# Packed attention and a low-rank MoE mixer on one core: GpSimd scales w1's high words, p is turned by plain products, and w2's first low part goes to VectorE

## The chip, the cores and the metric

The kernel runs on one core of a Trainium2 chip. The metric is the device time of one execution in microseconds (us); lower is better. A core has TensorE (matrix products, called PE in the profile, its weight loads PEld), VectorE (DVE), ScalarE (ACT), GpSimd (POOL) and SyncE (SP), which here issues nearly all transfers. Each engine works through its own queue in order; engines wait for each other and for transfers by semaphores.

## The reference, cut to what matters

```python
# q, k, v: (8, 8, 576, 64) float32   p: (8, 8, 32, 64) float32
p_packed = softmax(scale * p @ k^T) @ v            # 32 packed tokens per head
out      = softmax(scale * q @ p_packed^T) @ p_packed
x  = out as (8, 576, 512)
u  = x + (x^T @ U @ V)^T                           # U (576, 32), V (32, 576), float64 in memory
ch = max(u @ w_ch1, 0) @ w_ch2                     # w_ch1 (512, 2048), w_ch2 (2048, 512), float64 in memory
result = u + ch                                    # float32
```

The four weight arrays are float64 in memory. [...]

## The kernel before, in words

**Two parts.** The first part (lines 509 to 576, about the first 100 us) computes the packed attention of all 8 batches, converts w1 and does batch 0's second attention; a unit there is half a batch, four heads, and there are 16 units. Its instructions are put in order by the framework: with `schedule_with_timeline_sim=True` it simulates the program and gives each engine and each queue one fixed order. The second part (from line 579, `manual_schedule`) is the main loop. Its order is that in which the code is written. For each batch it goes over 16 tiles kt of the hidden width: `gemm1` (h_ps, with the folded first weight wth/wtl), the eviction with ReLU into a high and a low part (hh by ScalarE, hl by VectorE), and `gemm2` of the tile before (o, with w2h/w2l). Each product of these is three passes over high and low parts (`mm3`, L87 to L89). The bank of `h_ps` is single per half, so a tile's first product waits until the hl of the tile before has read it.

**w1.** 16 pieces of 128x512 are loaded by SP as pairs of words (`load_w1`, 512 KB each, four buffers, two named bits and two bits2), scaled (`test_w1`, L150, ScalarE: the high word read as a float32 and multiplied by 2 to the power of -112), and then shifted and joined by VectorE (`float32_of`, L80 to L82). `some_w1(n)` converts piece n, scales piece n+1 and loads piece n+4 into the buffer that n held. `fold` (L384) multiplies batch 0's packed tokens with w1; its results are evicted by ScalarE (wth, L390) and VectorE (wtl, L391).

**w2.** 16 tiles kt of 128x512, loaded into the two buffers `bits`, scaled by ScalarE (L79), joined by VectorE, and split into a high part (w2h, L165, ScalarE) and the rest (w2l, L166). Tiles 0, 1 and 2 are loaded late in the first part, tile 0 is converted and split there; its w2l is made by GpSimd, those of all other tiles by VectorE. The other tiles are converted between the steps of the main loop.

**p.** For each batch `a_load` brings p (pn, one buffer), and `a_p` turns it: GpSimd writes it twice side by side (pd, L433), TensorE transposes the two groups (L435), and ScalarE evicts them with the scale into pT: one copy for group 0 (L436), two for group 1, whose two halves change places within each pair of heads (L439). Then, for each unit: `a_turn` turns k (k_ps, kT), `a_scores` multiplies (L249, s_ps), `a_softmax` takes the maxima (L460, VectorE) and the exponentials (L462, ScalarE), `a_turn_back` turns them back (m_ps, eT, L471), `a_pack` multiplies with v (L490) and `a_heads` turns the result (L500). GpSimd also copies each result into ppall (L493) and does parts of the second attention (L290, L301, L347).

The order in which one unit is handled:

```python
a_turn_back(i - 1, ...); a_scores(i); a_load_v(i + 1); a_turn(i + 1); a_load(i + 2); a_softmax(i)
... some_w1(n_w1) ...
a_pack(i - 2, ...); a_heads(i - 3)
```

Of the kernel before, what the change touches and what calls it, by code (L numbers as in the profile page):

```python
# [9 lines left out]
F32 = mybir.dt.float32  # L10
F32R = mybir.dt.float32r
I32 = mybir.dt.int32
AF = mybir.ActivationFunctionType
ALU = mybir.AluOpType
# [6 lines left out]
def packed_attention_mixer_kernel(  # L21
# [27 lines left out]
    nc = tc.nc  # L49
    B, H, S, D = q.shape  # L50
# [4 lines left out]
    P = 128  # L55
# [7 lines left out]
    scale = 1.0 / float(D) ** 0.5  # L63
# [4 lines left out]
    REBIAS = 2.0 ** -112  # L68
    SIGN = -0x80000000

    U, V, w1, w2 = (a.bitcast(I32) for a in (U, V, w1, w2))
# [26 lines left out]

    ident = const.tile([P, P], F32, name="ident")
    make_identity(nc, ident)  # L100
    eps = const.tile([P, 1], F32, name="eps")
    nc.gpsimd.memset(eps, 1e-9)
    ppall = const.tile([P, B, 2, D], F32, name="ppall")
# [35 lines left out]
    bits = {}  # L139
# [6 lines left out]
    tests = {}  # L146

    def test_w1(n):
        tests[n] = conv_tile(F32)
        nc.scalar.activation(tests[n], bits["w1", n][:, :, 1].bitcast(F32), AF.Abs, scale=REBIAS)  # L150

    def convert_w1(n):
        x, c = chunks[n]
# [9 lines left out]
    def split_w2(kt, x):  # L163
        hi, lo = w2_parts(kt)
        nc.scalar.copy(hi, x)  # L165
        (nc.gpsimd if kt == 0 else nc.vector).tensor_tensor(lo, x, hi.bitcast(F32), op=ALU.subtract)  # L166

# [240 lines left out]
    def a_load(u):  # L410
        b, g = UN[u]
        ua[u] = {}
        if g == 0:
            pn[b] = sA.tile([P, 2, D], F32, name="pn", bufs=1)
            nc.sync.dma_start(out=pn[b], in_=p[b].rearrange("(g h) n d -> (h n) g d", g=2))
        ua[u]["x"] = sA.tile([P, 2 * S], F32, name="kx", bufs=3)
        load_nat(ua[u]["x"], k, b, g)
# [11 lines left out]
    def a_p(b):  # L429
        t_ps = bank()  # L430
        pT[b] = sA.tile([P, 2, P], F32, name="pT")
        pd = sA.tile([P, 2, 2, D], F32, name="pd", bufs=1)
        nc.gpsimd.tensor_copy(pd, pn[b].unsqueeze(2).to_broadcast([P, 2, 2, D]))  # L433
        for i in range(2):
            nc.tensor.transpose(t_ps[:, P * i:P * i + P], pd[:, i].rearrange("p z d -> p (z d)"), ident)  # L435
        nc.scalar.activation(pT[b][:, 0], t_ps[:, :P], AF.Copy, scale=scale)  # L436
        dst, src = (a.rearrange("p (y z n) -> p z y n", y=2, z=2) for a in (pT[b][:, 1], t_ps[:, P:2 * P]))
        for z in range(2):
            nc.scalar.activation(dst[:, z], src[:, 1 - z], AF.Copy, scale=scale)  # L439

    def a_turn(u):
        b, g = UN[u]
# [350 lines left out]
```

## Time and profile before

| | us |
|---|---|
| median of 3 runs | 831.68 (831.53 to 833.7) |
| the profiled execution | 831.53 |
| its span in the trace | 829.7 |
| TensorE busy | 798.7 |
| VectorE busy | 351.2 |
| ScalarE busy | 318.7 |
| GpSimd busy | 80.1 |
| first product of the main loop | 103.53 after the span's start |

The profile's page gives the busy time of each engine, a chain of waits followed back from the last instruction, and groups of equal instructions with their mean duration; `L87` is line 87 of the kernel before. Lines 101 to 432 of the kernel before have numbers higher by four in the kernel after (its L253 is L249 here), and from line 440 on they are the same. "x16" counts instructions; a plain float32 product leaves two of them in the trace. A view by stretches gives, for each stretch of time, the busy time of every engine, the clock that TensorE was granted (1.00 is full speed) and the share of time in which the 16 DMA engines worked.

### The profile page before, as it was taken

The page shows a single profiled execution, that of the slowest core. Times are in us where ns is not written, and L with a number is a line of the kernel's source. Part 1 is how long each engine was busy: PE and PEld are TensorE (multiplying, and loading weights), DVE is VectorE, ACT ScalarE, POOL GpSimd, SP SyncE. Part 2 cuts the span into 40 slices and gives each one's busy share as a digit, 9 for nine tenths or more (in the row PEclk, how much of TensorE's full clock was granted, in tenths as well). Part 3 has the DMA queues.
Part 4 walks back from the last instruction along what each step waited for, and adds up shares of the span by engine and source line. Part 5 has one row for each costly group of instructions (what it writes and reads, how often), then busy time and mean ns, then how long its engine had stood idle before and what let it go on. Part 6 is the DMA issues. An engine that isn't in the chain of part 4 may idle for free.

```text
span 829.7 us, 15436 instructions
## 1 busy us (share of the span) xinstructions
PE 798.7 (96%) x6224; PEld 643.7 (78%) x6224; DVE 351.2 (42%) x781; ACT 318.7 (38%) x974; POOL 80.1 (10%) x115
## 2 busy tenths in 40 slices
PE   7879698999999999999999999999999999999997
PEld 5556377888788888888888888888888888887886
DVE  3777467773343323433433234333434234332232
ACT  5788664354333332333333232343234232332231
POOL 0222201100111001010011001010101011100000
PEclk8999899999999999999999999999999999999999
DMA  9999764216001220023002120122002200030001
GB/s 299 347 360 358 252 139 127 78 51 188 1 1 47 100 55 2 1 96 92 1 1 89 58 55 2 46 87 57 2 18 90 73 22 1 14 111 1 2 0 64
DMA packets 60310, 70.23 MB, mean 85 GB/s; under 512 B 22864, under 2 KB 41296, under 8 KB 60240
## 3 DMA queue, kind: packets, MB, share of 16 engines
q1 hardware_dynamic: 59920, 68.73, 26.5%
q8 instruction: 49, 0.80, 0.4%
q10 hardware_dynamic: 320, 0.52, 0.2%
q14 instruction: 21, 0.17, 0.1%
HBM read 53.64 MB, written 15.60 MB: 83 GB/s over the span
## 4 chain that ended last, share of the span: by engine, by line
PE 89%; DVE 4%; DMA 3%; ACT 2%; issue 1%; POOL 0%; SPq 0%; ACTq 0%; POOLq 0%
PE o L87 16%; PE o L89 16%; PE o L88 16%; PE h_ps L87 9%; PE h_ps L89 8%; PE h_ps L88 8%; PE t_ps L384 4%; DMA bits<-in_moe_w_ch_dram 2%; PE o L654 2%; PE t_ps L229 2%; DMA vt<-in_v_dram 1%; PE t_ps L327 1%; PE t_ps L249 1%; PE t_ps L255 1%; DVE os L81 1%
## 5 line engine op out<-in xcount | busy, mean ns | idle before, releaser
L87 PE MATMUL o<-w2h,hh 128*128 128x512 f32 x512 | 206.6, 404 | 0.0
L89 PE MATMUL o<-w2h,hl 128*128 128x512 f32 x512 | 202.4, 395 | 0.0
L88 PE MATMUL o<-w2l,hh 128*128 128x512 f32 x512 | 201.9, 394 | 0.0
L637 DVE SCALAR_TENSOR_TENSOR hl<-h_ps,hh 128x256 fp32r<-128x256 f32 x256 | 105.4, 423 | 204.0 <-ACT hj L636 189.9
L634 ACT ACTIVATE hh<-h_ps 128x256 fp32r<-128x256 f32 x256 | 98.6, 386 | 182.9 <-PE h_ps L89 182.5
L87 PE MATMUL h_ps<-ah,wth 128*128 128x320 f32 (+1 forms) x512 | 157.7, 308 | 0.4 <-DVE hl L637 0.3
L88 PE MATMUL h_ps<-al,wth 128*128 128x320 f32 (+1 forms) x512 | 151.6, 296 | 0.0
L89 PE MATMUL h_ps<-ah,wtl 128*128 128x320 f32 (+1 forms) x512 | 151.5, 296 | 0.0
L87 PEld LDWEIGHTS h_ps<-ah,wth 128*128 128x128 f32 x512 | 96.7, 189 | 25.6 <-issue 21.0
L89 PEld LDWEIGHTS o<-w2h,hl 128*128 128x128 f32 x512 | 96.4, 188 | 22.5
L87 PEld LDWEIGHTS o<-w2h,hh 128*128 128x128 f32 x512 | 97.0, 189 | 21.0 <-issue 4.6
L88 PEld LDWEIGHTS o<-w2l,hh 128*128 128x128 f32 x512 | 97.0, 189 | 16.6
L88 PEld LDWEIGHTS h_ps<-al,wth 128*128 128x128 f32 x512 | 96.9, 189 | 1.9
L89 PEld LDWEIGHTS h_ps<-ah,wtl 128*128 128x128 f32 x512 | 97.0, 189 | 0.0
L391 DVE TENSOR_TENSOR wtl<-t_ps,wth 128x256 fp32r<-128x256 f32 x128 | 48.5, 420 | 102.4 <-ACT wth L390 99.0
L390 ACT CAST wth<-t_ps 128x256 fp32r<-128x256 f32 x128 | 43.3, 374 | 110.0 <-PE t_ps L384 102.3
L347 POOL TENSOR_TENSOR al<-aT,ah 128x320 fp32r<-128x320 f32 (+1 forms) x32 | 25.7, 806 | 211.5 <-ACT ah L346 211.5
L290 POOL TENSOR_TENSOR e<-e,m 128x576 f32<-128x576 f32 x16 | 18.6, 1160 | 261.8 <-DVE m L289 261.8
L236 ACT COPY xT<-t_ps 128x256 f32<-128x256 f32 x64 | 21.5, 395 | 38.9 <-PE t_ps L229 38.2
L384 PE MATMUL t_ps<-w1t,ppT 64*32 64x512 f32 x512 | 35.9, 615 | 0.0
L346 ACT CAST ah<-aT 128x320 fp32r<-128x320 f32 (+1 forms) x32 | 13.8, 435 | 43.8 <-DVE aT L345 43.8
L636 ACT ACTIVATE hj<-h_ps 128x64 f32<-128x64 f32 x128 | 28.3, 221 | 0.0
(121 smaller groups left out, 822.3 us busy)
## 6 DMA issues: line engine op xcount, KB each, us to landing
bits<-in_moe_w_ch_dram SPq DMA_DIRECT2D x32, 512.0 KB, 6.4
kx<-in_k_dram SPq DMA_DIRECT2D x16, 576.0 KB, 7.0
x<-in_q_dram SPq DMA_DIRECT2D x16, 576.0 KB, 5.0
vt<-in_v_dram SPq DMA_DIRECT2D x32, 256.0 KB, 6.9
out_dram<-bits SPq DMA_DIRECT2D x32, 256.0 KB, 2.4
aD<-aT SPq DMA_DIRECT2D x16, 288.0 KB, 2.1
aP<-aD SPq DMA_DIRECT2D x32, 128.0 KB, 3.4
ppP<-ppD SPq DMA_DIRECT2D x32, 64.0 KB, 3.1
```

Source lines behind the costliest of these rows:

```text
L87: nc.tensor.matmul(ps, lhsT=lh, rhs=rh, start=start, stop=False)
L88: nc.tensor.matmul(ps, lhsT=lh, rhs=rl, start=False, stop=False)
L89: nc.tensor.matmul(ps, lhsT=ll, rhs=rh, start=False, stop=stop)
L236: nc.scalar.copy(dst, src[:, a])
L290: nc.gpsimd.tensor_tensor(e, e, m.unsqueeze(2).to_broadcast([P, S // 32, 32]), op=ALU.subtract)
L347: nc.gpsimd.tensor_tensor(al[:, g, ns], aT[:, ns], ah[:, g, ns].bitcast(F32), op=ALU.subtract)
L384: nc.tensor.matmul(f_ps[g][xs], lhsT=ppT[b][zs, g, xs], rhs=w1t[h // 2][zs, QW * c:QW * c + QW], start=True, stop=True)
L390: nc.scalar.copy(hi[:, g], f_ps[g][:, cs])
L391: nc.vector.tensor_tensor(lo[:, g], f_ps[g][:, cs], hi[:, g].bitcast(F32), op=ALU.subtract)
L634: nc.scalar.activation(hh[:, ms], src, AF.Relu)
L636: nc.scalar.activation(hj[:, jslot(self.b, kt), self.js], h_ps[:, LAST], AF.Relu)
L637: nc.vector.scalar_tensor_tensor(hl[:, ms], src, 0.0, hh[:, ms].bitcast(F32), op0=ALU.max, op1=ALU.subtract)
```

## The change

Three edits, in the first part only. First, `test_w1` runs on GpSimd as a multiplication in place of ScalarE's absolute value with scale. The sign that this keeps is shifted out by the next step. Second, `a_p` no longer doubles and transposes p: it multiplies pn (as the stationary operand) with the identity for group 0 and with a new constant `swapped`, an identity with exchanged halves, for group 1, each once into the upper and once into the lower 64 rows of the bank; so the result stands in its final order and one ScalarE instruction evicts it. pd is gone and pn has two buffers. Third, w2's first low part is made by VectorE like the others.

```diff
+    swapped = const.tile([P, P], F32, name="swapped")
+    for z in range(2):
+        a, b = (x.rearrange("p (y z n) -> p z y n", y=2, z=2) for x in (swapped, ident))
+        nc.gpsimd.tensor_copy(a[:, z], b[:, 1 - z])
...
     def test_w1(n):
         tests[n] = conv_tile(F32)
-        nc.scalar.activation(tests[n], bits["w1", n][:, :, 1].bitcast(F32), AF.Abs, scale=REBIAS)
+        nc.gpsimd.tensor_single_scalar(tests[n], bits["w1", n][:, :, 1].bitcast(F32), REBIAS, op=ALU.mult)
...
     def split_w2(kt, x):
         hi, lo = w2_parts(kt)
         nc.scalar.copy(hi, x)
-        (nc.gpsimd if kt == 0 else nc.vector).tensor_tensor(lo, x, hi.bitcast(F32), op=ALU.subtract)
+        nc.vector.tensor_tensor(lo, x, hi.bitcast(F32), op=ALU.subtract)
...
-            pn[b] = sA.tile([P, 2, D], F32, name="pn", bufs=1)
+            pn[b] = sA.tile([P, 2, D], F32, name="pn", bufs=2)
...
     def a_p(b):
         t_ps = bank()
         pT[b] = sA.tile([P, 2, P], F32, name="pT")
-        pd = sA.tile([P, 2, 2, D], F32, name="pd", bufs=1)
-        nc.gpsimd.tensor_copy(pd, pn[b].unsqueeze(2).to_broadcast([P, 2, 2, D]))
-        for i in range(2):
-            nc.tensor.transpose(t_ps[:, P * i:P * i + P], pd[:, i].rearrange("p z d -> p (z d)"), ident)
-        nc.scalar.activation(pT[b][:, 0], t_ps[:, :P], AF.Copy, scale=scale)
-        dst, src = (a.rearrange("p (y z n) -> p z y n", y=2, z=2) for a in (pT[b][:, 1], t_ps[:, P:2 * P]))
-        for z in range(2):
-            nc.scalar.activation(dst[:, z], src[:, 1 - z], AF.Copy, scale=scale)
+        for i, z in product(range(2), range(2)):
+            nc.tensor.matmul(t_ps[D * z:D * z + D, P * i:P * i + P], lhsT=pn[b][:, i], rhs=(ident, swapped)[i],
+                             start=True, stop=True)
+        nc.scalar.activation(pT[b].rearrange("p g n -> p (g n)"), t_ps[:, :2 * P], AF.Copy, scale=scale)
```

Since the framework orders the first part anew, the edits move instructions on every engine. Three places follow. From the first product of the main loop on, the order of every engine is the same as before.

GpSimd's queue at the end of the first part, before (al is the low part of batch 0's second attention):

```order
L347 TENSOR_TENSOR al<-aT_918,ah 128x256
L347 TENSOR_TENSOR al<-aT_1122,ah 128x256
L493 COPY ppall<-two 128x64
L166 TENSOR_TENSOR w2l_103<-os,w2h_102 128x512
L433 COPY pd<-pn 128x256
```

and now:

```order
L154 TENSOR_SCALAR os<-bits_1410 128x512
L351 TENSOR_TENSOR al<-aT_911,ah 128x320
L493 COPY ppall<-two 128x64
L351 TENSOR_TENSOR al<-aT_1113,ah 128x320
L154 TENSOR_SCALAR os<-bits 128x512
L351 TENSOR_TENSOR al<-aT_911,ah 128x256
```

w2l and the copy of the last p, which stood behind it, are gone; the scaling of the last two pieces of w1 stands between the steps of al.

TensorE's queue around the last turning of p, before (unit 13's exponentials are e_1513, unit 12's are e_1413):

```order
L255 MATMUL m_ps<-ident,e_1513 128x128 x4
L257 MATMUL m_ps<-ident,e_1513 64x128
L490 MATMUL m_ps<-vt,eT 32x64 x20
L435 MATMUL t_ps<-ident,pd 128x128 x2
L500 MATMUL t_ps<-ident,two 128x128
L249 MATMUL s_ps<-kT,pT 32x320
```

and now (unit 12's exponentials are e_1402):

```order
L233 MATMUL k_ps<-ident,kx 128x128 x8
L500 MATMUL t_ps<-ident,two 128x128
L437 MATMUL t_ps<-ident,pn 64x128 x2
L437 MATMUL t_ps<-swapped,pn 64x128 x2
L259 MATMUL m_ps<-ident,e_1402 128x128 x4
L261 MATMUL m_ps<-ident,e_1402 64x128
```

The last p is turned one unit earlier, ahead of unit 12's transposes rather than behind those of unit 13. The first fold has moved forward too: its sixteen instructions, which stood between the scores and the transposes of unit 14, now stand in two halves, one ahead of and one among the scores of unit 14.

VectorE's queue at the end of the first part, before (L80 to L82 without w1t are w2's first tile; w1t is w1's last piece; L460 are the maxima of units 14 and 15):

```order
L80 TENSOR_SCALAR os<-os 128x512 x2
L81 SCALAR_TENSOR_TENSOR os<-bits,os 128x512 x2
L82 SCALAR_TENSOR_TENSOR os<-bits,os 128x512
L82 SCALAR_TENSOR_TENSOR w1t_101<-bits,os 128x512
L460 TENSOR_REDUCE sm<-s_ps 128x1
L478 RECIPROCAL sm<-sm 128x1
L391 TENSOR_TENSOR wtl<-t_ps,wth 128x256 x4
L460 TENSOR_REDUCE sm<-s_ps 128x1
```

and now:

```order
L80 TENSOR_SCALAR os<-os 128x512 x2
L460 TENSOR_REDUCE sm<-s_ps 128x1
L81 SCALAR_TENSOR_TENSOR os<-bits,os 128x512
L395 TENSOR_TENSOR wtl<-t_ps,wth 128x256
L81 SCALAR_TENSOR_TENSOR os<-bits,os 128x512
L82 SCALAR_TENSOR_TENSOR os<-bits,os 128x512
L478 RECIPROCAL sm<-sm 128x1
L82 SCALAR_TENSOR_TENSOR w1t_104<-bits,os 128x512
L395 TENSOR_TENSOR wtl<-t_ps,wth 128x256
L460 TENSOR_REDUCE sm<-s_ps 128x1
L170 TENSOR_TENSOR w2l_106<-os,w2h_105 128x512
```

The maxima of unit 14 now stand between the shifts and the joins of the two tiles; one of the fold's four evictions stands ahead of w1's last join and one behind it (the other two have moved ahead of these rows), and w2l closes them.

## The prediction

> **What bounds the kernel now.** I began with the page's first part (busy time of each engine), then cut the span into stretches.
>
> ```profile
> PE 798.7 (96%) x6224; PEld 643.7 (78%) x6224; DVE 351.2 (42%) x781; ACT 318.7 (38%) x974; POOL 80.1 (10%) x115
> ```
>
> TensorE is busy 96% of the span, so only its 31 us of idle time can be won. The view by stretches says where that lies.
>
> ```profile
> core 0: us, PE busy (x) PEld busy (x) DVE busy (x) ACT busy (x) POOL busy (x), PEclk, DMA share, GB/s
> 0.00:88.00 88.00, 71.85 (x1059) 49.48 (x1059) 57.49 (x119) 65.09 (x208) 18.34 (x38) 0.94 1.04 342
> 88.00:95.00 7.00, 2.25 (x55) 1.32 (x47) 3.66 (x8) 3.11 (x10) 1.56 (x3) 0.83 0.99 304
> 95.00:103.00 8.00, 6.07 (x85) 2.68 (x89) 3.00 (x7) 4.14 (x15) 0.51 (x2) 0.72 0.48 160
> 123.00:131.00 8.00, 5.80 (x45) 4.16 (x44) 6.38 (x13) 3.47 (x11) 0.24 (x1) 1.00 0.40 131
> 131.00:829.00 698.00, 693.19 (x4788) 570.46 (x4786) 266.99 (x607) 230.54 (x696) 58.93 (x70) 1.00 0.15 47
> ```
>
> From 131 us on TensorE idles 5 us in 698: that part runs by its own length, and what comes earlier only shifts it. Up to 88 us the DMA engines are full (share 1.04). Between 88 and 95 us nothing is: TensorE works 2.25 us of 7, every other engine about half or less. The chain of waits (start, length, what) shows who is waited for there.
>
> ```profile
> 89.12 0.24 POOL ppall L493
> 89.36 4.29 issue
> 93.68 1.25 POOL w2l L166
> 94.94 0.35 POOL pd L433
> 95.33 0.70 PE t_ps L435 x2
> ```
>
> GpSimd's queue holds w2's first low part (w2l) ahead of the doubled p (pd). w2l waits for a conversion that ends just before 93.68, so p's copy for the last batch, and with it TensorE, stands still for a tile that TensorE needs only in the main loop. TensorE's own rows (start, length, and in brackets the idle time before):
>
> ```profile
> 95.33 0.69 PE L435 MATMUL t_ps<-ident,pd 128*128 128x128 f32 x2 [4.62 <-POOL pd L433]
> 96.38 1.32 PE L249 MATMUL s_ps<-kT,pT 64*32 64x320 f32 x16 [0.15 <-ACT pT L436]
> 100.18 0.76 PE L249 MATMUL s_ps<-kT,pT 64*32 64x320 f32 x16
> 103.53 0.39 PE L87 MATMUL h_ps<-ah,wth 128*128 128x320 f32 x1
> 111.26 0.31 PE L87 MATMUL h_ps<-ah,wth 128*128 128x320 f32 x1
> 27.91 0.38 PE L435 MATMUL t_ps<-ident,pd 128*128 128x128 f32 x2
> ```
>
> The first product of the main loop starts at 103.53.
>
> **The change part by part.** *The stall.* After the change neither w2l nor any step of p is on GpSimd, and with two pn buffers the last p is loaded some twenty transfers sooner. In the trace of before it would have been there in time anyway:
>
> ```profile
> L415 SPq DMA_DIRECT2D pn<-in_p_dram x1: 373/373/373, 84.1 to 84.1; - x1
> DMA to landing us min/median/max: 6.6/6.6/6.6
> ```
>
> 84.1 + 6.6 = 90.7, just where the 4.62 us of idle time begin. All of it goes: −4.6.
>
> *What the stall slowed.* Behind it the granted clock is 0.72. The same two transposes take 0.69 there against 0.38 at 27.91, the same sixteen score products 1.32 against 0.76 at 100.18: 0.3 + 0.6, so −0.9.
>
> *The moved fold.* Its sixteen products now stand ahead, in two halves, and with them four evictions that ScalarE and VectorE did in turn:
>
> ```profile
> 101.97 0.59 ACT L471 COPY eT<-m_ps 128x512 f32<-128x512 f32 x1
> 99.98 0.27 PE L257 MATMUL m_ps<-ident,e 128*64 128x128 f32 x1
> ```
>
> The copy eT, which the last a_pack before the main loop waits for, could have begun at 100.3 and began at 101.97. Bounds 0 (one of the four is still just ahead of it) and 1.7; I take −1.0, since three of four have moved.
>
> *The new order on VectorE.* The shifts (L80) of w2's first and w1's last tile now stand ahead of the maxima of unit 14 (a half batch's packed attention), and wait for ScalarE's rescaling, which is itself behind the copy of eT for unit 13. Queued behind are the maxima; ScalarE's exponentials and TensorE's next transposes wait for those. From unit 13's transposes: eT 0.59, rescaling and two L80, against the score products that run in that time anyway.
>
> ```profile
> L80 DVE TENSOR_SCALAR os<-os 128x512 int32<-128x512 int32 x32 | 15.2, 476 | 7.5 <-ACT os L150 6.1 <-ACT os L79 1.2
> L150 ACT ACTIVATE os<-bits 128x512 f32<-128x512 f32 x16 | 11.0, 688 | 3.9 <-DMA bits<-in_moe_w_ch_dram 2.2 <-DVE os L80 1.8
> L439 ACT ACTIVATE pT<-t_ps 128x64 f32<-128x64 f32 x16 | 2.7, 226 | 0.0
> L436 ACT ACTIVATE pT<-t_ps 128x128 f32<-128x128 f32 x8 | 2.2, 277 | 7.4 <-PE t_ps L435 7.4
> L390 ACT CAST wth<-t_ps 128x256 fp32r<-128x256 f32 x128 | 43.3, 374 | 110.0 <-PE t_ps L384 102.3 <-DVE wtl L391 7.7
> L433 POOL COPY pd<-pn 128x256 f32<-128x256 f32 x8 | 4.0, 506 | 20.7 <-PE s_ps L249 11.8 <-DMA pn<-in_p_dram 8.9
> L199 POOL COPY x<-ident 128x512 f32<-128x512 f32 x1 | 1.4, 1427 | 0.3 <-DVE os L82 0.3
> ```
>
> 0.6 + 0.7 (the rescaling, by its like, L150) + 2 × 0.4 (L80's two overlap) is 2.1; scores and half a fold take 1.3 to 1.5 of it: +0.6.
>
> *ScalarE's relief.* It loses 16 × 0.69 = 11.0 us of scaling and, of p's evictions, 2.7 + 2.2 − 8 × 0.37 = 1.9: 13 us of the 65 that it works up to 88 us. There TensorE runs behind the landed data:
>
> ```profile
> L218 SPq DMA_DIRECT2D kx<-in_k_dram x1: 385/385/385, 75.8 to 75.8; - x1
> DMA to landing us min/median/max: 6.4/6.4/6.4
> 86.19 0.99 PE L229 MATMUL k_ps<-ident,kx 128*128 128x128 f32 x7
> ```
>
> The last k block lands at 75.8 + 6.4 = 82.2 and is turned at 86.2. Of these 4.0 us between none and all may come back; most waits there go round several engines, so I take −1.5.
>
> *What is added beside other work.* GpSimd gains 16 scalings of 128x512. Nearest rows: twice the 128x256 copy pd (2 × 0.4 undisturbed), 0.8, and the 128x512 copy at 1.43; I take 1.0, closer to pd as a plain one-input walk: 16 us onto 18.3 of 88, minus 4.0 for pd. TensorE turns each p by four plain products, two records each, in place of two transposes. Between the score products' pace (16 in 0.76, so 8 in 0.4) and the transposes' (2 in 0.38, so 8 in 1.5) that is 0 to +1.1 per p; I take +0.5, 4 us in all, under the DMA-bound stretch that leaves TensorE 16 us idle; without that cover it would be +4. Two copies for `swapped` come before TensorE's first turn. w2l costs VectorE one more 0.69, ready long before the second GEMM reads it. SP's queue moves the same bytes; its loads of p and w1 now wait for TensorE and GpSimd where they waited for GpSimd and ScalarE.
>
> The main loop's start thus moves by −4.6 − 0.9 − 1.0 + 0.6 − 1.5 = −7.4, to 96.1.
>
> **What is late next.** The third tile of the main loop's first GEMM (111.26) needs the bank that VectorE frees with the second tile's hl, and on ScalarE and VectorE that stands behind w2's second tile.
>
> ```profile
> L158 SPq DMA_DIRECT2D bits<-in_moe_w_ch_dram x2: 376/456/537, 94.1 to 94.7; - x2
> DMA to landing us min/median/max: 5.9/6.2/6.6
> 105.69 0.66 ACT L79 ACTIVATE os<-bits 128x512 f32<-128x512 f32 x1
> 109.56 0.75 DVE L637 SCALAR_TENSOR_TENSOR hl<-h_ps,hh 128x256 fp32r<-128x256 f32 x2
> 92.86 0.69 DVE L82 SCALAR_TENSOR_TENSOR w1t<-bits,os 128x512 int32<-128x512 int32 x1
> ```
>
> That tile lands at 94.1 + 5.9 = 100.0 and its conversion begins at 105.69; hl is done at 110.31, 4.62 later, with 0.95 to spare. So if w2's tile still lands at 100.0, the third GEMM tile can come 5.7 + 0.95 = 6.6 sooner and no more. Its load waits for w1's last conversion (L82, until 93.55), which now stands behind the maxima and a fold eviction on VectorE: 0 to 2.3 later, partly won back by the emptier DMA queue; I take 0.6. The gain is the smaller of 7.4 and 6.6 − 0.6: **6.0 us**. After that every engine's order is the same as before, so the shift passes to the end, the idle 2.2 us at 123 to 131 included. The profiled execution took 831.53 (span 829.7 and 1.8 around it), which gives 825.5; the median shown is 831.68, so I forecast **825.7**.
>
> **Rivals.** *The wait moves to w2's second tile.* For: its buffer is freed by VectorE, whose queue now waits for ScalarE and GpSimd at that place. Against: the gain is used up only by a landing 6.6 us later than now. If w1's last tile were converted 5 us later, w2's tile lands at about 104.9, and the gain is 1.7: 830.0.
>
> *GpSimd is late with w1, and SP's queue stands.* Each w1 load waits until an older tile is converted, and SP issues in order, so a late tile stops k and v too.
>
> ```profile
> 71.07 0.68 DVE L82 SCALAR_TENSOR_TENSOR w1t<-bits,os 128x512 int32<-128x512 int32 x1
> 71.98 0.41 SPq L144 DMA_DIRECT2D bits<-in_moe_w_ch_dram  x1
> L493 POOL COPY ppall<-two x15: 235/237/1118, 21.7 to 110.5; 128x64 f32<-128x64 f32 x15
> ```
>
> For: the tightest buffer is free only 0.2 us before its load, and GpSimd's small copy, 0.24 us as a rule, once took 1.12. Price: a tile is late by 0.3 (1.0 in place of 0.69) to 1.6 (1.43, and held up by 0.9 as that copy); 12 loads wait for a buffer, at 0.9 each 10.8 us. It decides once the stalls pass 6.0; in full, 831.5 − 6.0 + 10.8 = 836.3, slower. Against: a transfer lands 6 us after its issue, so an issue that is late by less still leaves the DMA engines work.
>
> The Trainium skill ("SBUF — State Buffer", section "SBUF: two separate sides") states a rule that speaks for this rival: GpSimd and a VectorE instruction with two SBUF inputs or in a two-port mode lock each other out for a whole instruction. The long copy agrees. By the rule alone 16 scalings hold VectorE up by at most 16 us, an estimate, against 30.5 us that it idles before 88 us, so the sum would stay.
>
> *More comes back.* All 4.0 us of the lag return and w2's tile lands 2.5 earlier: 823.0.
>
> **How the numbers follow.** Forecast 0.68, wait at w2's tile 0.16, GpSimd late 0.09, more 0.07. The forecast's own terms reach from a shift of 3 (second bounds of fold, lag and landing) to 8. Range 823.0 to 830.5: it leaves out the slower case and some of each edge. A measurement here tells 0.3%, 2.5 us, from no change. Faster (under 829.2): nearly all of the forecast, a quarter of the first rival and all of the last, 0.77; same 0.15; slower 0.08.
>
> **What would show it.** The idle 4.6 us ahead of the last turning of p are gone and the granted clock there is near 1; the first L87 starts at 95 to 98 (a start after 101 refutes the stall's cause); the third GEMM tile starts near 105 behind hl; the scaling takes 0.8 to 1.4 us on GpSimd; SP's issues of w1 wait for no conversion; from there on all rows keep their distances. A main loop that starts early while the end does not move would refute the last step.

## The result and the profile after

The changed kernel took 828.48 us (median, 827.05 to 830.46) beside 833.53 us for the kernel before on the same chip: a ratio of 0.9946, 95% interval 0.993 to 0.9962. Measured again in another group it was 827.52 beside 832.65, 0.9942 (0.9929 to 0.9954). So it is faster by 0.54 to 0.58%: 4.5 to 4.8 us by the ratios, 5.05 and 5.13 between the medians. In the two first traces the last product of the main loop ends at 825.34 before and at 821.66 after: 3.7 us earlier.

Engines' busy time, first part of the page, kernel after:

```profile
PE 802.1 (97%) x6272; PEld 645.7 (78%) x6272; DVE 352.8 (43%) x782; ACT 310.4 (38%) x942; POOL 101.8 (12%) x124
```

The same stretches as in the prediction, kernel after (columns as there):

```profile
0.00:88.00 88.00, 74.08 (x1062) 50.84 (x1063) 58.49 (x119) 55.61 (x174) 40.86 (x49) 0.96 1.03 342
88.00:95.00 7.00, 7.00 (x130) 3.93 (x128) 3.62 (x9) 5.74 (x20) 0.47 (x2) 1.00 0.85 258
95.00:103.00 8.00, 7.00 (x98) 5.51 (x91) 5.12 (x11) 5.26 (x16) 0.98 (x2) 1.00 0.69 222
111.00:123.00 12.00, 10.83 (x107) 8.00 (x106) 8.86 (x19) 6.93 (x21) 0.24 (x1) 1.00 0.82 191
```

The stretch from 88 to 95 us, in which TensorE worked 2.25 us of 7, is now full, at a clock of 1.00 in place of 0.83; from 95 to 103 the clock is 1.00 in place of 0.72. ScalarE has lost 9.5 us up to 88 us, GpSimd has gained 22.5. Between 111 and 123 us TensorE, busy 11.91 of 12 before, now idles 1.2; some 0.65 of that is only the idle time that ended at 127.76 before (1.77 us, for xT) and has moved ahead with everything else, and 0.43, ahead of the row at 111.48 below, is new.

TensorE's rows (start, length, and in brackets the idle time before), kernel after:

```profile
95.76 0.66 PE L259 MATMUL m_ps<-ident,e 128*128 128x128 f32 x4 [0.62 <-ACT e L462]
98.21 0.41 PE L87 MATMUL h_ps<-ah,wth 128*128 128x320 f32 x1
106.92 0.42 PE L87 MATMUL h_ps<-ah,wth 128*128 128x320 f32 x1 [0.75 <-DVE hl L637]
111.48 0.30 PE L261 MATMUL t_ps<-ident,e 128*64 128x128 f32 x1 [0.43 <-ACT xT L240]
```

The main loop starts at 98.21, 5.3 us earlier than before (103.53). The third tile of its first GEMM comes at 106.92, only 4.3 earlier (111.26): it waits 0.75 for hl. Behind 111.48, where the last unit is turned back, the lead is 3.6 and stays so to the end, give or take 0.1. In the second group's trace of the same kernel the start is 97.85, the third tile 105.87 and the end 820.58, so the loss at the third tile was 0.3 there, that at the turning back 0.6.

What is late is w2's second tile. VectorE's, SP's and ScalarE's rows, kernel after:

```profile
97.01 0.66 DVE L82 SCALAR_TENSOR_TENSOR w1t<-bits,os 128x512 int32<-128x512 int32 x1
97.22 1.02 SPq L162 DMA_DIRECT2D bits<-in_moe_w_ch_dram  x2
102.58 0.67 ACT L79 ACTIVATE os<-bits 128x512 f32<-128x512 f32 x1 [2.10 <-DMA bits<-in_moe_w_ch_dram]
```

The conversion that frees its buffer began at 92.86 and now begins at 97.01; its load went out at 94.11 and now at 97.22, although everything around it is earlier. It lands at 102.56, and ScalarE's scaling of it now waits 2.10 us for that; before, it began at 105.69, with the tile landed since 100.0.

GpSimd's scaling in the groups of instructions up to 90 us, kernel after:

```profile
L154 POOL TENSOR_SCALAR os<-bits 128x512 f32<-128x512 f32 x16 | 25.5, 1599 | 15.3 <-DMA bits<-in_moe_w_ch_dram 13.2 <-DVE w1t L82 1.9 <-issue 0.2
```

The waits of SP's queue up to 100 us (us in total, times, longest), kernel after:

```profile
SPq L148 <- DVE w1t L82: 5.4, 4, 2.2
SPq L148 <- POOL os L154: 1.3, 2, 1.0
```

A scaling takes 1.6 us on GpSimd, beyond my upper bound of 1.43, and SP's loads of w1 (L148) do wait for conversions, up to 2.2 us. My second rival's mechanism was thus there; it did not cost what the rival asked: the last k block still landed at 82.6 (82.2 before).

### The profile page after: what moved, and what is told of

Read it like the earlier page. It is cut to its first block, busy times and chain, and to the rows that moved or that the text cites. A ratio compares the mean times of both kernels' runs of the same rounds, so it can differ in the third digit from the quotient of the medians.

```text
span 826.5 us, 15498 instructions
## 1 busy us (share of the span) xinstructions
PE 802.1 (97%) x6272; PEld 645.7 (78%) x6272; DVE 352.8 (43%) x782; ACT 310.4 (38%) x942; POOL 101.8 (12%) x124
## 4 chain that ended last, share of the span: by engine, by line
PE 90%; DMA 5%; DVE 3%; ACT 1%; issue 1%; POOL 0%; SPq 0%; POOLq 0%; DVEq 0%; ACTq 0%
PE o L87 16%; PE o L89 16%; PE o L88 16%; PE h_ps L87 9%; PE h_ps L89 8%; PE h_ps L88 8%; PE t_ps L388 4%; DMA vt<-in_v_dram 2%; PE o L654 2%; DMA kx<-in_k_dram 2%; PE t_ps L233 2%; PE t_ps L253 1%; PE t_ps L331 1%; PE t_ps L259 1%; PE k_ps L233 1%; PE m_ps L490 1%
## 5 line engine op out<-in xcount | busy, mean ns | idle before, releaser
L395 DVE TENSOR_TENSOR wtl<-t_ps,wth 128x256 fp32r<-128x256 f32 x128 | 48.5, 419 | 103.5 <-ACT wth L394 100.1
L305 POOL TENSOR_TENSOR e<-e,s 128x576 f32<-128x576 f32 x16 | 19.4, 1216 | 93.6 <-DVE s L304 93.2
```

The source lines that it names most:

```text
L305: nc.gpsimd.tensor_tensor(e, e, s.unsqueeze(2).to_broadcast([P, S // 32, 32]), op=ALU.mult)
L395: nc.vector.tensor_tensor(lo[:, g], f_ps[g][:, cs], hi[:, g].bitcast(F32), op=ALU.subtract)
```

## The experiments

Three theories stand in the expectations. Theory 1 is the prediction's main term: the gain is the end of one stall, w2's first low part ahead of the last doubled p in GpSimd's queue. Theory 2: the gain is ScalarE's relief. Theory 3: GpSimd is too slow for w1 and gives some of it back. "Start" below is the start of the main loop; it was 103.53 in the trace of the kernel before.

The framework orders the first part of each of these kernels anew. In the traces, TensorE's instructions up to the main loop come in the same order in three groups: the kernel before and e_w2l; e_p and e_no_w1; the kernel after, e_no_w2l, e_turns and e_turns_pool. Between any other two, a difference holds the edit and another order together.

### One edit at a time

*e_w2l*, the kernel before with the third edit alone:

```diff
-        (nc.gpsimd if kt == 0 else nc.vector).tensor_tensor(lo, x, hi.bitcast(F32), op=ALU.subtract)
+        nc.vector.tensor_tensor(lo, x, hi.bitcast(F32), op=ALU.subtract)
```

> The kernel before with one edit: w2's first low part goes to VectorE; w1's scaling stays on ScalarE and p is still doubled on GpSimd. Theory 1 (the whole gain is GpSimd's queue, where w2's low part stood ahead of the last doubled p): the 4.62 us of idle time ahead of the last turning of p are gone (under 1 us left), the first product of the main loop starts at 98 to 99.5 (103.53 - 4.6 - 0.9, plus up to 0.7 for the low part on VectorE), and w2's second tile is loaded at 94 and lands at 100 as before, since what frees its buffer stands ahead of the stall. So nothing caps the gain: the third tile of the first GEMM at 106 to 107, and the time 4 to 5 us below the kernel before, as much as the whole change. Theory 2 (the gain is ScalarE's relief from scaling w1 and evicting p): ScalarE keeps all its work here, so the time is within 1 us of the kernel before.

Measured: 829.72 us, 0.9973 (0.9964 to 0.9983); start 100.54, 3.0 earlier, and the end moves by the same 3.0. SP's, GpSimd's and TensorE's rows of that kernel, and then one stretch of it:

```profile
84.71 0.37 SPq L415 DMA_DIRECT2D pn<-in_p_dram  x1
91.58 0.40 POOL L433 COPY pd<-pn 128x256 f32<-128x256 f32 x1 [2.86 <-DMA pn<-in_p_dram]
92.03 0.69 PE L435 MATMUL t_ps<-ident,pd 128*128 128x128 f32 x2 [1.96 <-POOL pd L433]
```

```profile
88.00:95.00 7.00, 4.11 (x72) 2.40 (x78) 4.74 (x10) 3.31 (x12) 0.87 (x3) 0.72 0.92 277
```

The stall shrinks from 4.62 to 1.96 and is not gone: behind w2's low part stood a second cause, p's own transfer, and the clock stays at 0.72. Theory 1 has its cause right and its size wrong: 3.0 of the 5.3 us, and a time 2.4 below the kernel before, not 4 to 5. Theory 2's "within 1 us" is out. Nothing is lost behind the start here, as expected: w2's second tile is loaded at 95.35, early enough.

*e_p*, the kernel before with the second edit alone (`swapped` as in the change):

```diff
-            pn[b] = sA.tile([P, 2, D], F32, name="pn", bufs=1)
+            pn[b] = sA.tile([P, 2, D], F32, name="pn", bufs=2)
...
-        pd = sA.tile([P, 2, 2, D], F32, name="pd", bufs=1)
-        nc.gpsimd.tensor_copy(pd, pn[b].unsqueeze(2).to_broadcast([P, 2, 2, D]))
...
+        for i, z in product(range(2), range(2)):
+            nc.tensor.matmul(t_ps[D * z:D * z + D, P * i:P * i + P], lhsT=pn[b][:, i], rhs=(ident, swapped)[i],
+                             start=True, stop=True)
+        nc.scalar.activation(pT[b].rearrange("p g n -> p (g n)"), t_ps[:, :2 * P], AF.Copy, scale=scale)
```

> The kernel before with one edit: p is turned by four plain products and evicted at once (with two pn buffers); w2's first low part stays on GpSimd and w1's scaling on ScalarE. Theory 1: no step of p is on GpSimd, so the low part holds nobody up: the idle time ahead of the last turning of p is gone and the first product of the main loop starts at 97 to 99.5. On VectorE the last w1 conversion now stands behind a unit's maxima and fold evictions, as in the changed kernel, so w2's second tile is loaded after 95.5 and lands at 101.5 to 103 (100.0 before), the third tile of the first GEMM comes at 106.5 to 107.5, and the time is 3 to 5 us below the kernel before. Theory 2: ScalarE loses 1.9 us of its 65 only, so the gain is under 1 us.

Measured: 829.72 us, 0.9968 (0.9956 to 0.998); start 101.72. The stall is gone (TensorE works 6.53 us of the 7 from 88 to 95), yet the start comes only 1.8 earlier, not the 4 to 6.5 expected, and the time is 2.4 below, not 3 to 5. Where the rest went no run separates: the order is another one, and in it the last k block is loaded at 82.06 us (75.80 before) and TensorE has worked 70.75 us up to 88 (71.85 before).

*e_w1*, the kernel before with the first edit alone:

```diff
-        nc.scalar.activation(tests[n], bits["w1", n][:, :, 1].bitcast(F32), AF.Abs, scale=REBIAS)
+        nc.gpsimd.tensor_single_scalar(tests[n], bits["w1", n][:, :, 1].bitcast(F32), REBIAS, op=ALU.mult)
```

> The kernel before with one edit: w1's high words are scaled by GpSimd. w2's low part and the doubled p both stay on GpSimd, but the order that comes out for GpSimd has the last doubled p ahead of w2's low part. Theory 1: with that order the 4.62 us of idle time are gone although nothing was taken off GpSimd; the scalings take 1.5 us each as in the changed kernel, and SP's w1 loads wait for conversions up to 2.2 us as there, so the gain is 2 to 5 us, no larger than the whole change's. Theory 2: ScalarE is relieved of 11 us here, and the gain is as large as the whole change's because of that: the lag of TensorE behind the last k block (4.0 us before) shrinks by 2 or more. Theory 3 (GpSimd is too slow for it): the 4 w1 loads that SP waits for cost what the stall gave back, and the time is within 1 us of the kernel before.

Measured: 832.14 us, 0.9997 (0.9988 to 1.0007); start 103.14. As the order had it, the doubled p now precedes w2's low part. GpSimd's rows, and then TensorE's at the second and at the last turning of p:

```profile
88.84 1.35 POOL L347 TENSOR_TENSOR al<-aT,ah 128x320 fp32r<-128x320 f32 x1 [4.69 <-ACT ah L346]
90.14 0.39 POOL L433 COPY pd<-pn 128x256 f32<-128x256 f32 x1
90.50 1.27 POOL L166 TENSOR_TENSOR w2l<-os,w2h 128x512 fp32r<-128x512 f32 x1
```

```profile
15.79 0.69 PE L435 MATMUL t_ps<-ident,pd 128*128 128x128 f32 x2 [3.23 <-POOL pd L433]
94.05 0.38 PE L435 MATMUL t_ps<-ident,pd 128*128 128x128 f32 x2
```

GpSimd waits 4.69 us at a low part of the second attention, which ScalarE delivers late, with p's copy behind it. But the copy is done at 90.53, and TensorE turns that p at 94.05 without any idle time before it. So the stall is gone here, and this wait is not what takes the gain. The time is lost earlier: up to 88 us TensorE has worked 67.15 us, 4.7 less than before. It waits 3.23 us for a doubled p at 15.79 (0.58 before), and from 80 to 88 us the transfers thin out; that stretch, and SP's longest wait from 74 to 92 us:

```profile
80.00:88.00 8.00, 6.49 (x128) 4.72 (x126) 5.62 (x12) 4.64 (x17) 1.71 (x3) 1.00 0.75 232
```

```profile
SPq L425 <- PE k_ps L239: 3.4, 1, 3.4
```

The share of the DMA engines is 0.75 there, against 1.07 before, and SP's queue stands 3.4 us at a load of v; the profile puts its release down to TensorE. Which of these made the loss no run separates. Theory 3's number holds (no gain), its mechanism is not shown. Theory 1 gave the order the whole gain: the wait it names is gone, and the time is not. Theory 2's 11 us of ScalarE do not show in the time either.

The rows of that kernel up to 90 us show one more thing:

```profile
L150 POOL TENSOR_SCALAR os<-bits 128x512 f32<-128x512 f32 x16 | 27.6, 1729 | 15.4 <-DMA bits<-in_moe_w_ch_dram 9.2 <-DVE x L320 3.1 <-DVE sm L478 2.4
L81 DVE SCALAR_TENSOR_TENSOR os<-bits,os 128x512 int32<-128x512 int32 x17 | 13.5, 797 | 0.3
L82 DVE SCALAR_TENSOR_TENSOR w1t<-bits,os 128x512 int32<-128x512 int32 x16 | 15.1, 943 | 0.3
```

VectorE's joins L81 and L82 were 0.70 and 0.69 us before. Singly, no 128x512 L82 beside which GpSimd was idle took over 0.69; those beside GpSimd's work reach 1.65. In sum L82 grows by 4.1 us, L81 by 1.6. In the changed kernel it is less: L81 means 0.793 and L82 0.698, 1.6 us in sum. The rule of the Trainium skill that the prediction weighed ("SBUF — State Buffer", section "SBUF: two separate sides": GpSimd and a VectorE instruction with two SBUF inputs exclude each other for a whole instruction) fits these rows.

### One part undone

*e_no_w1*, the kernel after with the first edit undone:

```diff
-        nc.gpsimd.tensor_single_scalar(tests[n], bits["w1", n][:, :, 1].bitcast(F32), REBIAS, op=ALU.mult)
+        nc.scalar.activation(tests[n], bits["w1", n][:, :, 1].bitcast(F32), AF.Abs, scale=REBIAS)
```

> The changed kernel with one part undone: w1's high words are scaled by ScalarE again; p's products and w2's low part on VectorE stay. Theory 1: the stall stays gone, and the time is within 1 us of the changed kernel (4 to 6 us below the kernel before). Theory 2: ScalarE has its 11 us back and most of the gain is lost: within 1.5 us of the kernel before. Theory 3 (the scaling on GpSimd, 1.5 us a piece in place of 0.69, delays w1's conversions and with them w2's second tile): the last w1 conversion ends 1 to 3 us earlier than in the changed kernel (97.67 there), the tile lands before 101.5 (102.56 there), and the time is 1 to 2 us below the changed kernel.

Measured: 829.34 us, 0.9963 (0.9952 to 0.9975); start 101.73, the same as with p's edit alone. It lies between the expectations: the stall is gone, and yet 3.5 to 3.9 us at the start come only with w1's move. Theory 3 is out for this kernel: w2's second tile was loaded at 97.43, no earlier than with GpSimd, and the time is above the changed kernel's, not below. For comparison the same kernel as changed was run again:

> The changed kernel itself, once more, beside the same runs of the kernel before as the variants of it in this group. Expected: 0.993 to 0.996 of the kernel before; first product of the main loop at 98.2, third tile of its first GEMM at 106.9, both within 0.3.

Measured: 0.9942 (0.9929 to 0.9954), start 97.85, third tile 105.87: the ratio as expected, the rows 0.36 and 1.05 earlier than in the first trace, more than the 0.3 I had allowed.

SP's rows of e_no_w1, and then of the kernel after, differ in the load of the last k block.

```profile
73.85 0.55 SPq L222 DMA_DIRECT2D kx<-in_k_dram  x1
81.38 0.39 SPq L222 DMA_DIRECT2D kx<-in_k_dram  x1
```

```profile
73.01 0.55 SPq L222 DMA_DIRECT2D kx<-in_k_dram  x1
74.56 0.38 SPq L222 DMA_DIRECT2D kx<-in_k_dram  x1
```

With the scaling on ScalarE the last k block goes out at 81.38, behind two units' v and a piece of w1; with the scaling on GpSimd at 74.56. Whether ScalarE's free time or only this other order matters was the next question.

*e_act_load*, the kernel after, in which ScalarE also does the old scaling, into a tile that is overwritten unread:

```diff
         nc.gpsimd.tensor_single_scalar(tests[n], bits["w1", n][:, :, 1].bitcast(F32), REBIAS, op=ALU.mult)
+        nc.scalar.activation(w2_parts(3)[1], bits["w1", n][:, :, 1].bitcast(F32), AF.Abs, scale=REBIAS)
```

> The changed kernel with ScalarE's relief alone taken away: w1's pieces are still scaled by GpSimd, and beside each scaling ScalarE does the old one too, into a tile of w2's low parts that nobody reads before it is overwritten (16 instructions of 0.69 us, work that nothing needs). Theory 'relief' (what w1's move brings, 3.5 to 3.9 us between the main loop's start at 101.73 without it and 97.85 to 98.21 with it, is ScalarE's 11 us, so that my term of 1.5 for it was too small): the start falls back to 100.5 to 102.5, the share of the DMA engines before 88 us to 1.02 or less, and the time to 0.996 to 0.998 of the kernel before. Rival 'place' (it is only the other order of loads and conversions that comes with the move): the start stays within 1 us of 98 and the time within 1 us of the changed kernel's.

Measured: 828.54 us, 0.9951 (0.9936 to 0.9965). A stretch of that kernel, and then SP's and TensorE's rows:

```profile
0.00:88.00 88.00, 74.54 (x1103) 49.90 (x1103) 61.42 (x120) 65.29 (x196) 44.37 (x49) 0.98 1.03 337
```

```profile
76.37 0.40 SPq L223 DMA_DIRECT2D kx<-in_k_dram  x1
96.22 0.42 PE L87 MATMUL h_ps<-ah,wth 128*128 128x320 f32 x1
98.57 0.34 SPq L163 DMA_DIRECT2D bits<-in_moe_w_ch_dram  x1
100.27 0.62 PE L87 MATMUL h_ps<-ah,wth 128*128 128x320 f32 x1 [2.19 <-DVE hl L638]
```

ScalarE is as busy as before the change (65.29 of 88 us; 65.09 then), and the main loop starts even earlier, at 96.22. So the early start does not need ScalarE's time, and theory 2 falls as its explanation. (This kernel has an order of its own too; what ScalarE's time would be worth in the changed kernel's order is not shown.) The rival's time, within 1 us of the changed kernel's, holds by the ratios; its start came 1.8 earlier than 98, 0.8 more than it allowed.

In this order the last k block is loaded at 76.37. That its place makes the start is argued, not shown: no run moved that load alone. Of the traces in which p is turned by products from two buffers, the six that load it at 74.6 to 76.4 start at 96.2 to 99.1, and the three that load it at 81.4 to 82.4 (e_p, e_no_w1 and e_stride) at 100.0 to 101.7; within the first group the order of the loads is not that of the starts. With p doubled on GpSimd the rule fails: 75.80 and 77.77 in the kernel before and e_w1, which start at 103.53 and 103.14.

The lead is lost again in this kernel, 7.3 at the start and 3.9 at the end. TensorE waits 2.19 us at the second GEMM tile for the first tile's hl. VectorE's rows, and then the stretch:

```profile
98.43 0.68 DVE L82 SCALAR_TENSOR_TENSOR w1t<-bits,os 128x512 int32<-128x512 int32 x1
99.19 0.69 DVE L171 TENSOR_TENSOR w2l<-os,w2h 128x512 fp32r<-128x512 f32 x1
99.80 0.75 DVE L638 SCALAR_TENSOR_TENSOR hl<-h_ps,hh 128x256 fp32r<-128x256 f32 x2
```

```profile
95.00:103.00 8.00, 5.81 (x71) 5.20 (x66) 5.37 (x11) 3.98 (x12) 0.61 (x1) 0.83 0.65 211
```

hl stands behind w1's last join and w2's first low part. Behind that wait the granted clock is low (0.83 in this stretch, 1.00 in the kernel after), and the first product takes 0.62 in place of 0.42. w2's second tile, loaded at 98.57, lands at 102.07, only after the wait.

*e_no_p*, the kernel before with the first and the third edit; p is doubled on GpSimd, and pn has one buffer:

```diff
-        nc.scalar.activation(tests[n], bits["w1", n][:, :, 1].bitcast(F32), AF.Abs, scale=REBIAS)
+        nc.gpsimd.tensor_single_scalar(tests[n], bits["w1", n][:, :, 1].bitcast(F32), REBIAS, op=ALU.mult)
...
-        (nc.gpsimd if kt == 0 else nc.vector).tensor_tensor(lo, x, hi.bitcast(F32), op=ALU.subtract)
+        nc.vector.tensor_tensor(lo, x, hi.bitcast(F32), op=ALU.subtract)
```

> The changed kernel with p's part undone: p is doubled on GpSimd and turned by two transposes, pn has one buffer; w1's scaling stays on GpSimd, w2's low part on VectorE. Theory 'one queue' (any step of p on GpSimd stands behind other work there that waits, whichever it is; with w1's scalings the doubled p stood behind a low part of the uv attention that waited 4.7 us for ScalarE): the main loop starts at 101.5 to 103.5, and the time is within 1.5 us of the kernel before. Theory 1 as first held (w2's low part alone is the stall): GpSimd has no low part of w2 any more, so the start is at 98 to 99.5 and the time 3.5 us or more below the kernel before.

Measured: 833.11 us, 1.0009 (0.9999 to 1.0019); start 104.56, 1.0 later than in the kernel before. TensorE's waits for a doubled p up to 112 us (us in total, times, longest), and then its rows at those two and at the last turning:

```profile
PE t_ps L435 <- POOL pd L433: 4.2, 2, 2.3
```

```profile
15.48 0.44 PE L435 MATMUL t_ps<-ident,pd 128*128 128x128 f32 x2 [2.33 <-POOL pd L433]
72.92 0.44 PE L435 MATMUL t_ps<-ident,pd 128*128 128x128 f32 x2 [1.88 <-POOL pd L433]
94.82 0.38 PE L435 MATMUL t_ps<-ident,pd 128*128 128x128 f32 x2
```

Two of three edits, and no gain, so theory 1 in its first form does not hold. But the waits are at earlier p's. The copy for the one at 15.48 waited for p's transfer, that for 72.92 stood on GpSimd behind a step of the second attention; at the last turning there is no wait. As in e_w1, SP's queue stands 3.4 us at a load of v, the share of the DMA engines from 80 to 88 us is 0.79, and up to 88 us TensorE has worked 69.42 us, 2.4 less than before. "One queue" has the time right, within 1.5 us of the kernel before, but the start lies beyond its 103.5, and only 1.88 us of the waits are of its kind. That p's copies on GpSimd make the loss is not shown.

*e_no_w2l*, the kernel after with the third edit undone:

```diff
-        nc.vector.tensor_tensor(lo, x, hi.bitcast(F32), op=ALU.subtract)
+        (nc.gpsimd if kt == 0 else nc.vector).tensor_tensor(lo, x, hi.bitcast(F32), op=ALU.subtract)
```

> The changed kernel with w2's first low part back on GpSimd; p's products and w1's scaling on GpSimd stay. Theory 'one queue' (the low part only hurts if a step of p stands behind it, and none is on GpSimd now): the start of the main loop within 0.6 of 98, and the time within 1 us of the changed kernel's, 0.993 to 0.996 of the kernel before. Rival (GpSimd is now too full, or the low part late for the second GEMM): the time 1 us or more above the changed kernel's.

Measured: 828.23 us, 0.9947 (0.993 to 0.9965), start 98.04: as the changed kernel, and TensorE's order is the same. The third edit does nothing that can be measured beside the other two.

*e_pn1*, the kernel after with one pn buffer:

```diff
-            pn[b] = sA.tile([P, 2, D], F32, name="pn", bufs=2)
+            pn[b] = sA.tile([P, 2, D], F32, name="pn", bufs=1)
```

> The changed kernel with one pn buffer in place of two; the order of all queues is as in the changed kernel. If the early load of p counts (with w2's low part alone moved, TensorE still waited 1.96 us for p's transfer, loaded at 84.7 and landed at 91.4): SP's queue waits at p's loads for the turning of the p before, the DMA engines' share before 88 us falls from 1.03 to 1.01 or less, the main loop starts at 99 to 101, and the time is 1 to 2.5 us above the changed kernel. If it doesn't (p's buffer is free by then anyway, since the products that free it come early): the start within 0.5 of 98.2 and the same time.

Measured: 830.32 us, 0.997 (0.9959 to 0.9981); start 100.66, 2.5 to 2.8 later, and half of the change's gain lost. Loads of the last p and TensorE's turning of it, first e_pn1, then the kernel after:

```profile
86.83 1.38 SPq L419 DMA_DIRECT2D pn<-in_p_dram  x1
93.05 0.44 PE L437 MATMUL t_ps<-ident,pn 128*64 128x128 f32 x4 [0.26 <-DMA pn<-in_p_dram]
```

```profile
64.48 0.41 SPq L419 DMA_DIRECT2D pn<-in_p_dram  x1
85.72 0.44 PE L437 MATMUL t_ps<-ident,pn 128*64 128x128 f32 x4
```

With one buffer fewer the last p is loaded at 86.8 in place of 64.5 and turned at 93.1 in place of 85.7. But the expectation is wrong that the order of all queues stays: w2's first two tiles are loaded at 74.70 and 88.32 (79.83 and 97.22 in the kernel after), the last k block at 77.91 (74.56), and TensorE's order is another. At the last turning itself TensorE waits 0.26 us for p. So the 2.5 to 2.8 us are the price of the buffer together with the order that comes with it; what p's lateness alone costs is not shown. The share of the DMA engines (1.02) decides nothing, as the changed kernel's own two traces have 1.03 and 1.01.

### The second tile of w2, and a better version

*e_turns*, the kernel after with another count of w1 conversions in the last units:

```diff
-    turns = [0, 0] + [1] * 10 + [2, 1, 2, 1]
+    turns = [0, 0] + [1] * 10 + [2, 2, 2, 0]
```

> The changed kernel with w1's last two conversions asked for one unit (a half batch's turn) earlier; nothing is left out or added. VectorE now converts w1's last piece before the last unit's maxima and fold evictions, and SP loads w2's second tile four loads earlier. Theory 'second tile' (1.0 of the 5.33 us won at the start of the main loop is lost again because w2's second tile is loaded at 97.2 and lands at 102.56): the tile is loaded before 95.5 and lands before 101, the 0.75 us of idle time ahead of the third GEMM tile are gone, that tile comes 7.7 us behind the first product as in the kernel before, and the end moves 0.8 to 1.7 us ahead of the changed kernel's. Rival 'the start pays for it' (VectorE does the conversion where the last units' maxima wait): the main loop starts 0.8 us or more later than at 98.2 and the time is that of the changed kernel or above. Rival 'the next wait takes it': the third tile comes early, but the copies of xT behind w2's conversions still cost theirs, and the end moves by under 0.5.

Measured: 826.31 us, 0.9916 (0.9903 to 0.9929), in the same group as the 827.52 of the changed kernel. VectorE's, SP's and TensorE's rows:

```profile
90.17 0.69 DVE L82 SCALAR_TENSOR_TENSOR w1t<-bits,os 128x512 int32<-128x512 int32 x1
90.92 0.33 SPq L162 DMA_DIRECT2D bits<-in_moe_w_ch_dram  x1
99.10 0.41 PE L87 MATMUL h_ps<-ah,wth 128*128 128x320 f32 x1
106.86 0.31 PE L87 MATMUL h_ps<-ah,wth 128*128 128x320 f32 x1
```

w2's second tile goes out at 90.92, six us sooner. The third GEMM tile comes 7.76 behind the first product (7.73 before, 8.71 and 8.02 in the two traces after), without a wait, and the 0.7 at the turning back are not lost either: the lead of 4.4 us at the start is the lead at the end. TensorE's order is that of the changed kernel, so the tile's landing was the cap. The start paid for part of it, 99.10 against 97.85 to 98.21, so that both this theory and its first rival are partly right. It is the fastest of the kernels run. Its interval only touches that of the changed kernel, and its profiled execution ends at 820.91, between the 820.58 and 821.66 of the changed kernel's two: that it beats the kernel before is measured, that it beats the change by 1.2 us rests on two medians.

*e_turns_pool*, e_turns with the third edit undone:

```diff
-        nc.vector.tensor_tensor(lo, x, hi.bitcast(F32), op=ALU.subtract)
+        (nc.gpsimd if kt == 0 else nc.vector).tensor_tensor(lo, x, hi.bitcast(F32), op=ALU.subtract)
```

> The version with w1's last conversions one unit earlier (0.9916 of the kernel before), and w2's first low part on GpSimd in place of VectorE. If VectorE's queue at the end of the first part still sets the time, its 0.7 us for the low part come back: 0.3 to 0.8 us below that version. If not: the same within 0.3 us and the main loop starts at 98.5 to 99.5.

Measured: 827.25 us, 0.9933 (0.9918 to 0.9948), start 98.17. The start is 0.9 us earlier than in e_turns, and earlier than the 98.5 to 99.5 of the second case, but the time is not lower. In this trace the lead is 5.4 us at the start, 5.3 at the third GEMM tile and 4.4 at the end. What is lost is lost in this stretch:

```profile
123.00:131.00 8.00, 8.00 (x42) 6.35 (x35) 6.18 (x13) 2.29 (x7) 1.16 (x1) 0.79 0.53 146
```

The granted clock is 0.79 there (1.00 in e_turns). So taking the low part off VectorE does move the start, and in this trace a lower clock takes it back. Whether it does so in the runs without a trace is not shown; over a whole run the granted clock was 0.992 to 0.996 here and 0.995 to 1.000 in e_turns.

### The price of a scaling on GpSimd

*e_stride*, the kernel after with three multiplications ahead of w1's first scaling (L522 to L524):

```diff
+    half, full = w1t[3][:, :512], w1t[3][:, :1024].rearrange("p (x t) -> p x t", t=2)
+    nc.gpsimd.tensor_single_scalar(w1t[3][:, :1024].rearrange("p (y n) -> p y n", n=P), ident.unsqueeze(1).to_broadcast([P, 8, P]), 2.0, op=ALU.mult)
+    nc.gpsimd.tensor_single_scalar(w1t[2][:, :512], half, 2.0, op=ALU.mult)
+    nc.gpsimd.tensor_single_scalar(w1t[2][:, 512:1024], full[:, :, 1], 2.0, op=ALU.mult)
     test_w1(0)
```

> The changed kernel with three more multiplications on GpSimd ahead of w1's first scaling, into parts of the w1 tiles that are overwritten later: one of 1024 elements a partition that reads a 128-wide tile over and over, one of 512 from consecutive words, one of 512 from every second word, as the scaling reads w1's high words. Only their durations are wanted; the time of the whole is not compared. Theory 'stride' (I took 1.0 us for a scaling, it took 1.54, because it reads every second word): the consecutive one takes 0.7 to 1.1 us, the other 1.4 to 1.6. Rival 'operation' (a multiplication of fp32 on GpSimd costs 3 ns an element however it is read): both take 1.4 to 1.6, and the one of 1024 about twice that.

GpSimd's rows of that kernel:

```profile
2.12 2.77 POOL L522 TENSOR_SCALAR w1t<-ident 128x1024 f32<-128x1024 f32 x1
4.98 1.49 POOL L523 TENSOR_SCALAR w1t<-w1t 128x512 f32<-128x512 f32 x1
6.43 1.53 POOL L524 TENSOR_SCALAR w1t<-w1t 128x512 f32<-128x512 f32 x1
```

1.49 and 1.53: how the words are read hardly matters, and 1024 elements take nearly twice as long. The operation costs 2.7 to 3.0 ns an element, about as the 128x512 copy of L199 did (1427 ns, 2.8 each), and not 1.6 as the copies pd (0.4 us for 256), by which I had priced it. The rival is right that the way of reading is not the cause; why pd is cheaper no run shows.

The same trace holds something that was not asked of it. SP's and TensorE's rows:

```profile
82.39 0.42 SPq L222 DMA_DIRECT2D kx<-in_k_dram  x1
99.99 0.41 PE L87 MATMUL h_ps<-ah,wth 128*128 128x320 f32 x1
```

All three edits are in this kernel, and ScalarE is as free as in the changed one (55.53 us busy up to 88, 55.61 there). Three instructions more on GpSimd in the first 8 us gave another order, the last k block went out 7.8 us later, and the main loop starts 1.8 to 2.1 us later. The added 5.8 us of GpSimd's time are in this too, so it is a hint, not a proof, that the order of the loads counts.

## Why the prediction was right, and where its steps were wrong

The forecast was 825.7, the median 828.48 and then 827.52, inside the range, and faster by more than 0.3%. The miss of 1.8 to 2.8 has two parts: the kernel before itself took 832.65 to 833.53 in these groups, not 831.68, which is 1.0 to 1.85; and the gain between the medians was 5.05 and 5.13 in place of 6.0.

That the sum came so near is in part luck: two of its terms are far off in opposite directions. In e_no_w1 the stall and the low clock behind it are gone, priced together at −5.5, and the start is 1.8 earlier; w1's move, priced at −1.5, then brings 3.5 to 3.9.

**The stall.** That it would go was right (the row with 4.62 us idle has no successor; the clock is 1.00). The step "in the trace of before it would have been there in time anyway", with two pn buffers costed at nothing, was wrong. p landed at 90.7, just when TensorE fell idle, and that was read as in time; it is the next limit. "Between 88 and 95 us nothing is" full was the same slip: the row above it has the DMA engines at a share of 0.99 there. With w2's low part gone and p loaded as before, 1.96 us of idle time and the low clock remain (e_w2l: 3.0 won, not 4.6 + 0.9). Taking the second buffer away costs 2.5 to 2.8, with the other order that it brings (e_pn1). The stall goes in whole because the change contains both.

**ScalarE's relief, −1.5.** The name does not hold (e_act_load starts early without that relief), and the size is too small: w1's move is worth 3.5 to 3.9 at the start once p is off GpSimd, 0.4 alone, and it costs 4.0 beside w2's edit alone (100.54 to 104.56). By what the traces show it comes with another order of loads, which is argued and not isolated; I had read the order around the stall and not that of the loads at 74 to 81 us.

**The start.** −7.4 was forecast, −5.3 and −5.7 came; 95 to 98 was the sign, 98.2 and 97.85 the rows. Whether the terms for the moved fold (−1.0) and the new order on VectorE (+0.6) took the difference, no run separates.

**What is late next.** The mechanism was right: the third tile behind hl, behind w2's second tile, shown by e_turns. The term was mis-sized: "0 to 2.3 later, I take 0.6" measured 3.1 and 2.75 for the load (97.22 and 96.86 against 94.11), beyond its bound, and 2.5 and 1.5 for the landing (102.56 and 101.50 against 100.04). The prediction's rule, 6.6 less that lateness, would give 4.1 and 5.1; the third tile came 4.3 and 5.4 earlier. So the first rival's wait came in part, with 1.0 and 0.3 us lost at the third tile. The row that I had quoted for it, L82 at 92.86, now begins at 97.01.

**"From there on all rows keep their distances."** Right from about 115 us on, but one more 0.7 us is lost at the turning back of the last unit. It is absent where w2's second tile lands early (e_turns), which speaks for the same cause.

**Side terms.** The scaling at "1.0, closer to pd", with 1.4 as the upper end: 1.5 to 1.6. "SP's issues of w1 wait for no conversion": they wait 5.4 us in four places; the DMA engines' share stays at 1.03 (1.04 before), so that seems to cost little. TensorE's four products for a p, taken as +0.5, last 0.7 us, from 85.72 to 86.38, against the 0.4 of two transposes. The range: by the prediction's own rule (the smaller of the start's shift and the cap) its second bounds give a shift of 4.3, not 3, at the low end, and 6.6, not 8, at the high one.

## What to carry to other kernels

When a wait is removed, look up what lands just as the wait began: a transfer that arrives at the moment an engine falls idle is not in time, it is the next limit, and taking one buffer away there cost about as much here (2.5 to 2.8 us, its other order included) as the removal alone had brought (3.0). Edits around one in-order queue do not add: alone they were worth 0.4, 1.8 and 3.0 us at the start, the first and third together −1.0, the second and third 1.8, the first and second 5.5, all three 5.3 to 5.7; so price the set, and undo each part to see which of them carry it. And where a framework orders the program, compare the order of every queue over the whole stage, not only around the stall, before a difference is put down to an edit: three instructions added for a measurement moved the main loop here by 1.8 to 2.1 us.

## What the runs showed of the hardware that was not expected

A multiplication of fp32 by a constant on GpSimd took 1.49 us for 128x512 from consecutive words and 1.53 from every second word (2.77 for 128x1024), almost four times pd's 0.4 us for half the elements, by which it was priced. And VectorE's two-input joins of 128x512, 0.69 us each, were stretched up to 1.65 where GpSimd worked beside them, 5.7 us in sum in the kernel with w1's move alone.
